# One more Sinkhorn column sum in a fused attention and mixture-of-experts kernel, with the third group of y multiplied one phase later and W2's splits three products later

## The chip, the cores and the metric

The kernel runs on one NeuronCore of a Trainium2 chip, in one launch. The metric is the device time of one execution in microseconds (us); what is shown is the median of several executions. The profile is that of one execution.

## The reference

```python
# linear attention: 4 batches, 8 heads, 768 steps, head size 48
for t in range(S):
    cur = np.einsum('bhd,bhe->bhde', u[None] * kt, vt)
    y[:, :, t] = np.einsum('bhd,bhde->bhe', rt, state + cur)
    state = wt[:, :, :, None] * state + np.einsum('bhd,bhe->bhde', kt, vt)
...
x = np.ascontiguousarray(attn_out.transpose(0, 2, 1, 3)).reshape(B * S, H * D)  # 3072 tokens x 384
a = x @ w1
b = x @ w2
h = a * b @ w3
x = h @ w_out
...
N, D = x.shape
E = w_gate.shape[1]                          # 8 experts, F = 1024
logits = x @ w_gate
logits = logits - logits.max()
P = np.exp(logits)
for _ in range(8):
    P /= P.sum(1, keepdims=True) + 1e-09     # rows
    P /= P.sum(0, keepdims=True) + 1e-09     # columns
    P *= N / E
out = np.zeros((N, D), dtype=np.float32)
for e in range(E):
    h = np.maximum(x @ w1[e], 0.0)
    ye = h @ w2[e]
    out += P[:, e:e + 1] * ye
```

## The kernel before

The attention and the first gated layers take the first 440 us. The rest, the eight experts, is what the change touches. It is cut into 64 phases n = 4k + sb: sb is one of four blocks of 768 tokens, k one of 16 pairs of 128-column slices of the hidden layer (an expert e has two such pairs, e = k // 2). `phase(n)` computes x @ w1 of its slice and block; the second multiplication, with w2, of phase n follows inside phase n + 1, and a 65th phase has only that.

**The first multiplication** (tile `zp`) is done by a scheme that needs 15 products instead of a full set of block products. They come in the order 8, 9, 10, 5, 2, 13, 11, 6, 3, 15, 12, 7, 1, 14, 4. Numbers are split into a high and a low part (fp32r), so a product is 6 matmuls: 128 x 128 weights, 256 moving columns. Around the products ScalarE copies some out of PSUM (L1015, `ct`: that of product 8 must be done before product 9 goes on in the same bank), VectorE adds and subtracts (L1008, L1011), ScalarE makes the high part of relu(.) (L1000, `hh`) and VectorE its low part (L1005, `hl`).

**The second multiplication** (tile `yp`, "y") of a phase has 36 steps of 3 matmuls of the same shape. Three groups b_ = 0, 2, 1 (a group is one 256-column part of the block's tokens) have twelve steps each, and fill two PSUM banks of three. `y_out` adds a finished bank to the accumulator: for e > 0 VectorE multiplies it by the transposed token weights (`yw`, L1191; `pb` is a row of them, broadcast), and GpSimd adds it (L1193). For the first expert it is copied or added without the weights, which are not known yet, and in phases 8 to 11 `rescale` (L1276) multiplies the accumulator by them afterwards.

**What sets the order.** The schedule is written out by hand: each engine runs its instructions in the order in which the program issues them. `after(r)` runs behind each product: tasks that are due, one entry of the list `ex`, at products 2, 4, 6, 8 and 10 of a phase one entry of the list `sk`, and then a number of y steps given by a table (5, 4, 0, 5, 4, 0, 2, 1, 2, 1, 3, 3, 2, 1, the rest). `ex` holds what comes one for a product: the rescalings, and in phases with sb = 2 the splits of two new w2 slices (L740 on ScalarE for the high part, L741 on VectorE for the low one). `sk` holds the Sinkhorn iteration in small pieces, over phases 1 to 7:

```python
def sk_cols():
    pc = pools["y"].tile([P, E], F32, tag="col", name="pcs")
    mm(pc, so["ones"], so["cs"], True, True)
```

is the column sum of one iteration, a plain fp32 matmul with 8 moving columns on TensorE (two instructions in the trace); eight of them fall into phases 2 to 6, and two transposes (`ptn`) of the token weights follow in phase 7. Every matmul of the kernel goes through one helper, L113, so the tiles' names tell them apart.

Of the kernel before, what the change touches and what calls it, by code (L numbers as in the profile page):

```python
# [11 lines left out]
F32 = mybir.dt.float32  # L12
# [46 lines left out]
def tile_rwkv_moe_sinkhorn_moe(  # L59
# [21 lines left out]
    P = 128  # L81
    FF = moe_w3.shape[0] * P
    E = e_w2.shape[0] * 2 * P // FF
# [10 lines left out]
    KD = DM // P  # L94
# [89 lines left out]
    pools = {}  # L184
# [682 lines left out]
    for k in range(NC):  # L867
# [9 lines left out]
        if k + 2 < NC:  # L877
            n = FU + 2 * k + 4
# [80 lines left out]
    so = {}  # L959
# [78 lines left out]
    def phase(n):  # L1038
        z = n < N
        bk, ct = {}, {}  # L1040

        def prod(nm, r, start=False, stop=False):
            if start:
                bk[nm] = z_new()
            z_prod(bk[nm], n, r, start, stop)

        def after(r):
            if ORDER.index(r) % 4 == 3 or r == ORDER[-1]:
                release(n, GOF[r])
            while at["slot"] in due:  # L1050
                for f in due.pop(at["slot"]):
                    f()
            at["slot"] += 1
            if ex:
                ex.popleft()()
            if sk and at["sk"] and ORDER.index(r) in SKP:
                sk.popleft()()
            if n == 0:
                i_ = ORDER.index(r)
                if i_ < PO:  # L1060
                    moe_x2(NB - 1, i_, PO, PARTS[i_:i_ + 2])
                if i_ == PO - 1:
                    open2()
                if i_ == 11:
                    y_fill(0)
                y_units((0, 0, 3, 3, 6)[max(0, i_ - 10)])
            elif n == 1:
                y_units(YN1[r])
            else:
                y_units(YN[r])  # L1070

        def s8():
            prod("b", 8, True, True)
            ct["8"] = cp(bk["b"])

        def s9():
            prod("b", 9, False, True)
            ct["12"] = cp(bk["b"])

        def s10():  # L1080
            prod("b", 10, False, True)
            ct["02"] = cp(bk["b"])

        def s5():
            prod("a", 5, True, True)
            ct["01"] = new_c()
            sub(ct["01"], bk["a"], ct["02"])

        def s2():
            prod("a", 2, False, True)  # L1090
            sub(ct["8"], bk["a"], ct["8"])

        def s13():
            prod("a", 13, False, True)
            ct["00"] = cp(bk["a"])

        def s11():
            prod("g", 11, True, True)
            sub(ct["02"], ct["02"], bk["g"])

        def s6():
            prod("e", 6, True, True)
            ct["10"] = new_c()
            add(ct["10"], ct["00"], bk["e"])

        def s3():
            prod("g", 3, False, True)
            add(ct["00"], ct["00"], bk["g"])

        def s15():  # L1110
            prod("f", 15, True, True)
            sub(ct["10"], ct["10"], bk["f"])
            h_hi(n, 1, 0, ct["10"])
            add(ct["12"], ct["12"], bk["f"])

        def s12():
            prod("h", 12, True, True)
            add(ct["00"], ct["00"], bk["h"])
            h_hi(n, 0, 0, ct["00"])
            h_lo(n, 1, 0)  # L1120

        def s7():
            prod("e", 7, False, True)
            add(ct["8"], ct["8"], bk["e"])
            h_hi(n, 1, 1, ct["8"])
            h_lo(n, 0, 0)

        def s1():
            prod("h", 1, False, True)
            add(ct["12"], ct["12"], bk["h"])  # L1130
            h_lo(n, 1, 1)

        def s14():
            prod("d", 14, True, True)
            add(ct["02"], ct["02"], bk["d"])
            h_hi(n, 0, 2, ct["02"])
            add(ct["12"], ct["12"], bk["d"])
            h_hi(n, 1, 2, ct["12"])

        def s4():  # L1140
            prod("i", 4, True, True)
            add(ct["01"], ct["01"], bk["i"])
            h_hi(n, 0, 1, ct["01"])
            h_lo(n, 0, 2)

        for r, f in zip(ORDER, (s8, s9, s10, s5, s2, s13, s11, s6, s3, s15, s12, s7, s1, s14, s4)):
            if z:
                f()
            after(r)
        if z:  # L1150
            h_lo(n, 1, 2)
            h_lo(n, 0, 1)

    pbc = {}

    def ld_pb(e, sb):
        t = pools["m2"].tile([P, S], F32, tag="pb", bufs=4, name="pb")
        nc.sync.dma_start(t, pd.rearrange("(e t) c -> e (t c)", e=E)[e, sb * S:(sb + 1) * S].partition_broadcast(P))
        pbc[e, sb] = t

    def y_fill(n):
        k, sb = divmod(n, NS)
        e, dp = divmod(k, NDP)
        bank = {}

        def unit(b_, d, i, j):
            first = i == 1 and j == 0
            last = i == 0 and j == 1
            if first and d != 1:
                bank[b_, d // 2] = pools["y"].tile([P, 2, T], F32, tag="y", bufs=3, name="yp")  # L1170
            yp = bank[b_, d // 2]
            hh, hl = hb[n, i, b_]
            wh, wl = w2c[2 * k + j]
            for c, (w_, a_) in enumerate(((wh, hh), (wh, hl), (wl, hh))):
                mm(yp[:, d % 2, :], w_[:, i, d * P:(d + 1) * P], a_[:, j, :], first and c == 0 and d != 1,
                   last and c == 2, skip=True)
            if last and d:
                y_out(yp[:, 0:d % 2 + 1, :], b_, slice(0, 2) if d == 1 else slice(2, 3))

        def y_out(yp, b_, ds):  # L1180
            if k == 0 and sb not in acc:
                acc[sb] = pools["x"].tile([P, KD, S], F32, tag="xa", bufs=NS, name="acc")
            dst = acc[sb][:, ds, b_ * T:(b_ + 1) * T]
            w_ = ds.stop - ds.start
            if k == 0:
                nc.scalar.activation(dst, yp, AF.Copy)
            elif e == 0:
                add(dst, yp, dst)
            else:
                t = pools["m2"].tile([P, w_, T], F32, tag=f"yw{w_}", name="yw")  # L1190
                nc.vector.tensor_tensor(t, yp, pbc[e, sb][:, b_ * T:(b_ + 1) * T].unsqueeze(1).to_broadcast([P, w_, T]),  # L1191
                                        op=ALU.mult)
                (nc.vector if n == N - 1 else nc.gpsimd).tensor_tensor(dst, dst, t, op=ALU.add)  # L1193
            if k == NB2 - 1:
                nc.sync.dma_start(out.rearrange("(d p) t -> p d t", p=P)[:, ds, sb * S + b_ * T:sb * S + (b_ + 1) * T], dst)

        for b_ in (0, 2, 1):
            for d in range(KD):
                for i in (1, 0):
                    for j in range(2):  # L1200
                        yq.append(lambda b_=b_, d=d, i=i, j=j: unit(b_, d, i, j))

    def release(n, g):
        if n >= N:
# [63 lines left out]
        nc.vector.tensor_copy(so["pt"][:, h, :], pt)  # L1268
        nc.sync.dma_start(pd[PH * h:PH * (h + 1), :], so["pt"][:, h, :])

    sk.extend([sk_last, lambda: sk_turn(0), lambda: sk_turn(1), lambda: ld_pb(0, 0)])

    def rescale(sb, d, h):
        ts_ = slice(h * S // 2, (h + 1) * S // 2)
# [8 lines left out]
    for n in range(N + 1):  # L1283
        k, sb = divmod(n, NS)
        if n > 1:
            y_fill(n - 1)
        if n < N:
            if n == 0:
                for m, at_ in enumerate(sorted(hook)):
                    later(m, *hook[at_])  # L1290
                later(4, lambda: sp_w2(0))
                later(6, lambda: sp_w2(1))
                for r, (d0, d1, d2, sb_, ws) in XAT.items():
                    task = lazy(lambda r=r, sb_=sb_, ws=ws: pre_x(NS - 1, r, x2[sb_], ws, nc.gpsimd))
                    for d, f in zip((d0, d1, d2), task):
                        later(d, f)
            if 2 * NS <= n < 3 * NS:
                ex.extend([lambda sb=sb, d=d, h=h: rescale(sb, d, h) for d in range(KD) for h in range(2)])
                if sb < NS - 1:
                    later(2, lambda sb=sb: ld_pb(0, sb + 1))  # L1300
            if n >= 2 * NS:
                later(3, lambda n=n: ld_pb(n // NS // NDP, n % NS))
            if n == 2:
                for g in range(NGR):
                    later(3 * g + 7, lambda g=g: spread(0, 5, sp_w1(2, g, nc.gpsimd)))
            if sb == 1 and k > 0:
                for g in range(NGR):
                    later(3 * g + 1, lambda i=2 * k + 2, g=g: spread(0, 2, sp_w1(i, g, nc.gpsimd)))
            if sb == 2:
                ex.extend([lambda i=i: sp_w2(i) for i in (2 * k + 2, 2 * k + 3)])  # L1310
        at["sk"] = n >= 1
        phase(n)
# [72 lines left out]
```

## Time and profile before

| | |
|---|---|
| median of 3 executions | 1942.75 us (1942.31 to 1945.38) |
| the profiled execution, its own time | 1941.5 us |
| its span | 1939.8 us |
| granted TensorE clock, mean | 1.00 |
| TensorE busy | 1913.2 us, 99% of the span |
| VectorE busy | 1400.1 us, 72% |
| GpSimd busy | 1020.2 us, 53% |
| ScalarE busy | 690.9 us, 36% |

The span is the time from the first to the last instruction of the profiled execution; it lies 1.7 us below that execution's own time. Busy shares are means over the whole program; a matmul's record overlaps with those of its neighbours, so the pace of TensorE is read from the distances between the starts.

### The profile page before, as it was taken

Reading aid. Unit: us, or ns where it says so; the run is one execution under the profiler, and the core shown is the slowest. Engines: PE = TensorE matmul, PEld = TensorE weight load, DVE = VectorE, ACT = ScalarE, POOL = GpSimd, SP = SyncE. Lnnn points to the kernel's source line nnn. Section 1 sums busy time; section 2 is a strip of 40 time slices with the busy share of each in tenths; the row PEclk is TensorE's granted clock in tenths of the full one; section 3 lists DMA queues with packets and bytes.
Section 4 is the critical chain, followed back from the end, with each engine's and each line's share of the span. In section 5 each row is a group of like instructions: output and inputs, shape, how many; then the busy total and the mean of one; then the engine's idle time right before and its main releaser. Section 6 shows DMA issues by size and latency. Waiting matters only on the chain.

```text
span 1939.8 us, 44922 instructions
## 1 busy us (share of the span) xinstructions
PE 1913.2 (99%) x18451; PEld 1879.3 (97%) x18451; DVE 1400.1 (72%) x2424; ACT 690.9 (36%) x1366; POOL 1020.2 (53%) x1245
## 2 busy tenths in 40 slices
PE   6999999999999999999999999999999999999999
PEld 4799999999999999999999999999999999999999
DVE  8866778766687877676767676767677777767666
ACT  6733343445432333333333333333333333323321
POOL 6867666545422455555555545464646464555521
PEclk9999999999999999999999999999999999999999
DMA  9632445349555665565655565556565655555564
GB/s 374 226 106 64 153 132 154 103 146 319 186 208 180 226 222 205 195 218 191 217 188 204 194 219 196 205 198 215 189 218 199 209 201 197 205 192 210 183 212 134
DMA packets 102733, 377.90 MB, mean 195 GB/s; under 512 B 11552, under 2 KB 39040, under 8 KB 76928
## 3 DMA queue, kind: packets, MB, share of 16 engines
q1 hardware_dynamic: 101664, 374.59, 55.0%
q8 instruction: 145, 2.38, 0.5%
q10 hardware_dynamic: 864, 0.44, 0.1%
q14 instruction: 60, 0.49, 0.1%
HBM read 353.26 MB, written 20.55 MB: 193 GB/s over the span
## 4 chain that ended last, share of the span: by engine, by line
PE 92%; DVE 3%; DMA 1%; ACT 1%; POOL 1%; issue 1%; SPq 0%; ACTq 0%; DVEq 0%; POOLq 0%
PE yp L113 41%; PE zp L113 34%; PE po L113 5%; PE pb L113 4%; PE pa L113 4%; PE w34ps L113 1%; PE yt L113 1%; PE sc L113 1%; DMA nat_kn<-in_kn_dram 1%; PE trn L113 0%; DMA raw<-in_moe_w_dram 0%; DVE ct L1008 0%; DMA xraw<-xraw 0%; DVE Sn L456 0%; DVE tx L673 0%
## 5 line engine op out<-in xcount | busy, mean ns | idle before, releaser
L113 PE MATMUL zp<-xc,w1c 128*128 128x256 f32 x5760 | 812.9, 281 | 0.8 <-DVE ct L1008 0.7
L113 PEld LDWEIGHTS zp<-xc,w1c 128*128 128x128 f32 x5760 | 737.4, 189 | 1.4 <-DVE ct L1008 0.9
L1193 POOL TENSOR_TENSOR acc<-acc,yw 128x512 f32<-128x512 f32 x330 | 362.2, 1098 | 561.8 <-DVE yw L1191 558.5
L113 PE MATMUL yp<-hh,w2h 128*128 128x256 f32 x2304 | 647.8, 281 | 0.0
L113 PE MATMUL yp<-hl,w2h 128*128 128x256 f32 x2304 | 647.0, 281 | 0.2 <-DVE hl L1005 0.2
L113 PE MATMUL yp<-hh,w2l 128*128 128x256 f32 x2304 | 646.8, 281 | 0.0
L113 PEld LDWEIGHTS yp<-hh,w2l 128*128 128x128 f32 x2304 | 441.4, 192 | 0.0
L113 PEld LDWEIGHTS yp<-hh,w2h 128*128 128x128 f32 x2304 | 432.9, 188 | 0.2 <-issue 0.2
L113 PEld LDWEIGHTS yp<-hl,w2h 128*128 128x128 f32 x2304 | 432.5, 188 | 0.5 <-DVE hl L1005 0.4
L1000 ACT ACTIVATE hh<-ct 128x512 fp32r<-128x512 f32 x384 | 236.1, 630 | 539.5 <-DVE ct L1011 272.8
L1008 DVE TENSOR_TENSOR ct<-ct,zp 128x512 f32<-128x512 f32 x576 | 381.1, 679 | 41.0 <-PE zp L113 37.7
L1005 DVE SCALAR_TENSOR_TENSOR hl<-ct,hh 128x512 fp32r<-128x512 f32 x384 | 314.6, 833 | 0.0
L1015 ACT ACTIVATE ct<-zp 128x512 f32<-128x512 f32 x256 | 152.5, 596 | 446.3 <-PE zp L113 446.3
L1191 DVE TENSOR_TENSOR yw<-yp,pb 128x512 f32<-128x512 f32 x336 | 185.6, 552 | 85.7 <-issue 22.1
L1011 DVE TENSOR_TENSOR ct<-ct,zp 128x512 f32<-128x512 f32 x128 | 87.9, 687 | 166.9 <-PE zp L113 166.9
L681 POOL TENSOR_TENSOR w1c<-w1s,w1c 128x512 fp32r<-128x512 f32 (+1 forms) x120 | 127.8, 1065 | 101.9 <-ACT w1c L677 101.9
L1011 DVE TENSOR_TENSOR ct<-zp,ct 128x512 f32<-128x512 f32 x128 | 88.3, 690 | 117.0 <-PE zp L113 101.0
L673 POOL TENSOR_TENSOR w1s<-w1raw 128x128 f32<-128x128 f32 x240 | 127.0, 551 | 0.2
L545 POOL TENSOR_TENSOR gl<-gs,gh 128x256 fp32r<-128x256 f32 (+1 forms) x88 | 81.2, 926 | 78.7 <-ACT gh L541 78.5
L113 PE MATMUL pb<-xhl,w2h 128*128 128x256 f32 (+1 forms) x528 | 103.9, 291 | 1.3 <-DVE gs L536 0.9
L113 PE MATMUL pa<-xhl,w1h 128*128 128x256 f32 (+1 forms) x528 | 102.7, 289 | 1.7 <-ACT w34s L263 1.0
L681 POOL TENSOR_TENSOR w1c<-w1raw,w1c 128x128 fp32r<-128x128 f32 (+1 forms) x93 | 59.0, 635 | 66.6 <-ACT w1c L677 64.9
(197 smaller groups left out, 2116.3 us busy)
## 6 DMA issues: line engine op xcount, KB each, us to landing
xc<-xd SPq DMA_DIRECT2D x192, 1024.0 KB, 4.9
xc<-xd SPq DMA_DIRECT2D x64, 768.0 KB, 4.3
pb<-pd SPq DMA_DIRECT2D x60, 384.0 KB, 5.7
xd<-x2s SPq DMA_DIRECT2D x54, 256.0 KB, 2.7
w1raw<-in_e_w_dram SPq DMA_DIRECT2D x32, 384.0 KB, 3.1
w2raw<-in_e_w_dram SPq DMA_DIRECT2D x32, 384.0 KB, 3.7
raw<-in_moe_w_dram SPq DMA_DIRECT2D x8, 1024.0 KB, 8.6
nat_w<-in_w_dram SPq DMA_DIRECT2D x24, 264.5 KB, 3.7
```

Source lines behind the costliest of these rows:

```text
L113: nc.tensor.matmul(o, lhsT, rhs, start=start, stop=stop, **kw)
L545: nc.gpsimd.tensor_tensor(gl[:, f, :], m_t.pop(("gs", blk, f)), gh[:, f, :].bitcast(F32), op=ALU.subtract)
L673: eng.tensor_tensor(tmp_[:, many.index(r), :], at_(a), at_(b), op=ALU.add if sg == 1 else ALU.subtract)
L681: eng.tensor_tensor(lo[:, d0:d1, :], sv, hi[:, d0:d1, :].bitcast(F32), op=ALU.subtract)
L1000: nc.scalar.activation(hh, src, AF.Relu)
L1005: nc.vector.scalar_tensor_tensor(hl, src, 0.0, hh.bitcast(F32), op0=ALU.max, op1=ALU.subtract)
L1008: nc.vector.tensor_tensor(o, a, b_, op=ALU.add)
L1011: nc.vector.tensor_tensor(o, a, b_, op=ALU.subtract)
L1015: nc.scalar.activation(t, src, AF.Copy)
L1191: nc.vector.tensor_tensor(t, yp, pbc[e, sb][:, b_ * T:(b_ + 1) * T].unsqueeze(1).to_broadcast([P, w_, T]), op=ALU.mult)
L1193: (nc.vector if n == N - 1 else nc.gpsimd).tensor_tensor(dst, dst, t, op=ALU.add)
```

## The change

Three things are done. One: a piece `sk_edge` is added at the end of `sk`. It is one more column sum, the same matmul as in `sk_cols` into a tile that nobody reads; it stands behind the two transposes and the load of the first broadcast weights, in phase 7 behind product 6. Two: the results of the third group (b_ = 1) of y(n) are not handed to `y_out` in phase n + 1, where the group is computed, but kept, and taken behind products 8 and 9 of phase n + 2; the steps of that group are sorted so that the three d of i = 1 come before those of i = 0. Three: `ex` gets three empty entries ahead, so that the rescalings stand behind products 5 to 3 instead of 8 to 13, and the two W2 splits behind products 5 and 2 instead of 8 and 9 (in phase 10, where the rescalings are ahead of them, behind 15 and 12 instead of 11 and 6).

On TensorE in phase 7 of the changed kernel (`zp` the products, `yp` the y steps, `pcs` the new sum; the numbers are those of the weights' buffers):

```order
L113 MATMUL yp<-hl,w2h_7526 128x256
L113 MATMUL yp<-hh,w2l_7527 128x256
L113 MATMUL zp<-xc_8861,w1c_7641 128x256 x3
L113 MATMUL zp<-xc_8861,w1c_7918 128x256 x3
L113 MATMUL pcs<-cs,ones 128x8
L113 MATMUL yp<-hh,w2h_7494 128x256
```

The sum stands between the six matmuls of product 6 and the y step that follows it; the rows around it are in before in the same order.

On VectorE at the end of one of the later phases and the start of the next, before (`yw` is the multiplication by the weights, `ct` the additions around the products, `hl` the low parts):

```order
L1008 TENSOR_TENSOR ct<-ct,zp 128x512
L1005 SCALAR_TENSOR_TENSOR hl<-ct,hh 128x512
L1191 TENSOR_TENSOR yw<-yp,pb 128x512
L1008 TENSOR_TENSOR ct<-ct,zp 128x512 x3
L1005 SCALAR_TENSOR_TENSOR hl<-ct,hh 128x512
L1191 TENSOR_TENSOR yw<-yp,pb 128x256
L1005 SCALAR_TENSOR_TENSOR hl<-ct,hh 128x512 x2
L1191 TENSOR_TENSOR yw<-yp,pb 128x512
L1011 TENSOR_TENSOR ct<-zp,ct 128x512
```

and the same place after the change:

```order
L1008 TENSOR_TENSOR ct<-ct,zp 128x512
L1005 SCALAR_TENSOR_TENSOR hl<-ct,hh 128x512
L1008 TENSOR_TENSOR ct<-ct,zp 128x512 x3
L1005 SCALAR_TENSOR_TENSOR hl<-ct,hh 128x512 x3
L1198 TENSOR_TENSOR yw<-yp,pb 128x512
L1198 TENSOR_TENSOR yw<-yp,pb 128x256
L1198 TENSOR_TENSOR yw<-yp,pb 128x512
L1011 TENSOR_TENSOR ct<-zp,ct 128x512
```

The two multiplications of the third group (a wide and a narrow one) stood ahead of the last additions and among the low parts; they now stand behind all of these, next to the first multiplication of the new phase.

On VectorE in phase 10, before (`acc` the rescalings, `w2l` the low parts of the W2 splits):

```order
L1276 TENSOR_TENSOR acc<-acc,pb 128x384 x2
L1011 TENSOR_TENSOR ct<-ct,zp 128x512
L741 TENSOR_TENSOR w2l_10072<-w2raw,w2h_10071 128x768
L1191 TENSOR_TENSOR yw<-yp,pb 128x512
L1008 TENSOR_TENSOR ct<-ct,zp 128x512
L741 TENSOR_TENSOR w2l_10098<-w2raw,w2h_10097 128x768
```

and after:

```order
L1289 TENSOR_TENSOR acc<-acc,pb 128x384
L1011 TENSOR_TENSOR ct<-ct,zp 128x512
L1008 TENSOR_TENSOR ct<-ct,zp 128x512
L741 TENSOR_TENSOR w2l_10123<-w2raw,w2h_10122 128x768
L1198 TENSOR_TENSOR yw<-yp,pb 128x256
L1008 TENSOR_TENSOR ct<-ct,zp 128x512
L1005 SCALAR_TENSOR_TENSOR hl<-ct,hh 128x512
L741 TENSOR_TENSOR w2l_10147<-w2raw,w2h_10146 128x768
```

The rescalings reach further into the phase, and the two low parts of W2 stand three products later, among the additions that end in h. The diff:

```diff
--- before.py
+++ after.py
@@ -1045,6 +1045,8 @@
             z_prod(bk[nm], n, r, start, stop)
 
         def after(r):
+            if r in ORDER[:2] and kept:
+                kept.popleft()()
             if ORDER.index(r) % 4 == 3 or r == ORDER[-1]:
                 release(n, GOF[r])
             while at["slot"] in due:
@@ -1152,6 +1154,7 @@
             h_lo(n, 0, 1)
 
     pbc = {}
+    kept = deque()
 
     def ld_pb(e, sb):
         t = pools["m2"].tile([P, S], F32, tag="pb", bufs=4, name="pb")
@@ -1175,7 +1178,11 @@
                 mm(yp[:, d % 2, :], w_[:, i, d * P:(d + 1) * P], a_[:, j, :], first and c == 0 and d != 1,
                    last and c == 2, skip=True)
             if last and d:
-                y_out(yp[:, 0:d % 2 + 1, :], b_, slice(0, 2) if d == 1 else slice(2, 3))
+                f = lambda: y_out(yp[:, 0:d % 2 + 1, :], b_, slice(0, 2) if d == 1 else slice(2, 3))
+                if b_ == 1 and n < N - 1:
+                    kept.append(f)
+                else:
+                    f()
 
         def y_out(yp, b_, ds):
             if k == 0 and sb not in acc:
@@ -1195,10 +1202,12 @@
                 nc.sync.dma_start(out.rearrange("(d p) t -> p d t", p=P)[:, ds, sb * S + b_ * T:sb * S + (b_ + 1) * T], dst)
 
         for b_ in (0, 2, 1):
-            for d in range(KD):
-                for i in (1, 0):
-                    for j in range(2):
-                        yq.append(lambda b_=b_, d=d, i=i, j=j: unit(b_, d, i, j))
+            pieces = [(d, i) for d in range(KD) for i in (1, 0)]
+            if b_ == 1 and n < N - 1:
+                pieces.sort(key=lambda x: -x[1])
+            for d, i in pieces:
+                for j in range(2):
+                    yq.append(lambda b_=b_, d=d, i=i, j=j: unit(b_, d, i, j))
 
     def release(n, g):
         if n >= N:
@@ -1268,7 +1277,11 @@
         nc.vector.tensor_copy(so["pt"][:, h, :], pt)
         nc.sync.dma_start(pd[PH * h:PH * (h + 1), :], so["pt"][:, h, :])
 
-    sk.extend([sk_last, lambda: sk_turn(0), lambda: sk_turn(1), lambda: ld_pb(0, 0)])
+    def sk_edge():
+        pc = pools["y"].tile([P, E], F32, tag="col", name="pcs")
+        mm(pc, so["ones"], so["cs"], True, True)
+
+    sk.extend([sk_last, lambda: sk_turn(0), lambda: sk_turn(1), lambda: ld_pb(0, 0), sk_edge])
 
     def rescale(sb, d, h):
         ts_ = slice(h * S // 2, (h + 1) * S // 2)
@@ -1295,6 +1308,7 @@
                     for d, f in zip((d0, d1, d2), task):
                         later(d, f)
             if 2 * NS <= n < 3 * NS:
+                ex.extend([lambda: None] * 3)
                 ex.extend([lambda sb=sb, d=d, h=h: rescale(sb, d, h) for d in range(KD) for h in range(2)])
                 if sb < NS - 1:
                     later(2, lambda sb=sb: ld_pb(0, sb + 1))
@@ -1307,6 +1321,8 @@
                 for g in range(NGR):
                     later(3 * g + 1, lambda i=2 * k + 2, g=g: spread(0, 2, sp_w1(i, g, nc.gpsimd)))
             if sb == 2:
+                if not ex:
+                    ex.extend([lambda: None] * 3)
                 ex.extend([lambda i=i: sp_w2(i) for i in (2 * k + 2, 2 * k + 3)])
         at["sk"] = n >= 1
         phase(n)
```

## Rows read from the trace of the kernel before

**Rows 1.** The page, busy time by engine (part 1) and costliest group (part 5).

```profile
PE 1913.2 (99%) x18451; PEld 1879.3 (97%) x18451; DVE 1400.1 (72%) x2424; ACT 690.9 (36%) x1366; POOL 1020.2 (53%) x1245
...
L113 PE MATMUL zp<-xc,w1c 128*128 128x256 f32 x5760 | 812.9, 281 | 0.8 <-DVE ct L1008 0.7
```

**Rows 2.** The chain of waits, two neighbouring phases: start us, us, what.

```profile
758.02 1.77 PE yp L113 x15
...
781.35 1.77 PE yp L113 x15
```

**Rows 3.** Timeline of TensorE, phase 5: start us, us, engine, line, operation, tiles, shapes.

```profile
558.38 0.28 PE L113 MATMUL yp<-hh,w2h 128*128 128x256 f32 x1
...
572.20 0.28 PE L113 MATMUL yp<-hh,w2l 128*128 128x256 f32 x1
```

**Rows 4.** Three windows: us; busy us of PE, PEld, DVE, ACT, POOL (records); clock; DMA.

```profile
559.00:572.00 13.00, 13.00 (x117) 13.00 (x117) 12.80 (x25) 4.72 (x11) 8.05 (x14) 1.00 0.64 228
584.00:596.00 12.00, 12.00 (x104) 12.00 (x103) 10.94 (x20) 4.17 (x7) 0.00 (x0) 1.00 0.68 234
758.02:781.35 23.33, 23.33 (x201) 23.33 (x200) 18.14 (x30) 8.13 (x14) 6.46 (x6) 1.00 0.66 224
```

**Rows 5.** Timeline of TensorE around three column sums and a transpose, phases 2 to 7.

```profile
488.02 0.29 PE L113 MATMUL pcs<-cs,ones 128*128 128x8 f32 x2
...
488.95 0.28 PE L113 MATMUL yp<-hh,w2h 128*128 128x256 f32 x1
...
503.57 0.28 PE L113 MATMUL pcs<-cs,ones 128*128 128x8 f32 x2
...
503.91 0.28 PE L113 MATMUL yp<-hl,w2h 128*128 128x256 f32 x1
...
513.34 0.29 PE L113 MATMUL pcs<-cs,ones 128*128 128x8 f32 x2
...
596.87 0.27 PE L113 MATMUL ptn<-ident,L 128*96 128x128 f32 x1
```

**Rows 6.** Timeline at the start of phase 6: VectorE, ScalarE, weight load [idle before <- releaser].

```profile
567.82 1.21 DVE L1005 SCALAR_TENSOR_TENSOR hl<-ct,hh 128x512 fp32r<-128x512 f32 x1
...
568.95 0.68 DVE L1008 TENSOR_TENSOR acc<-yp,acc 128x512 f32<-128x512 f32 x1
...
571.34 0.68 DVE L1005 SCALAR_TENSOR_TENSOR hl<-ct,hh 128x512 fp32r<-128x512 f32 x1
...
571.99 0.58 ACT L1015 ACTIVATE ct<-zp 128x512 f32<-128x512 f32 x1
...
572.62 0.19 PEld L113 LDWEIGHTS zp<-xc,w1c 128*128 128x128 f32 x1 [0.34 <-ACT ct L1015]
```

**Rows 7.** Timeline of phase 18: ScalarE and TensorE at its start, VectorE at its end.

```profile
852.03 0.58 ACT L1015 ACTIVATE ct<-zp 128x512 f32<-128x512 f32 x1
...
852.91 0.87 PE L113 MATMUL zp<-xc,w1c 128*128 128x256 f32 x6
...
871.63 0.69 DVE L1191 TENSOR_TENSOR yw<-yp,pb 128x512 f32<-128x512 f32 x1
```

**Rows 8.** Timeline of VectorE in phase 18, and TensorE's product 13.

```profile
856.72 0.69 DVE L1011 TENSOR_TENSOR ct<-zp,ct 128x512 f32<-128x512 f32 x1
857.77 0.42 DVE L1191 TENSOR_TENSOR yw<-yp,pb 128x256 f32<-128x256 f32 x1 [0.37 <-PE yp L113]
859.12 0.69 DVE L1011 TENSOR_TENSOR ct<-zp,ct 128x512 f32<-128x512 f32 x1 [0.92 <-PE zp L113]
...
860.33 0.64 PE L113 MATMUL zp<-xc,w1c 128*128 128x256 f32 x4
```

**Rows 9.** Timeline of ScalarE and VectorE in phase 10, the splits of W2.

```profile
675.22 1.57 ACT L740 ACTIVATE w2h<-w2raw 128x768 fp32r<-128x768 f32 x2
...
676.09 0.96 DVE L741 TENSOR_TENSOR w2l<-w2raw,w2h 128x768 fp32r<-128x768 f32 x1
```

**Rows 10.** Timeline of VectorE in phase 6, the first of four small Sinkhorn operations.

```profile
577.42 0.35 DVE L1245 TENSOR_TENSOR Pm<-Pm,cs 128x192 f32<-128x192 f32 x1
```

## The prediction

> **What bounds the kernel now.** I read the engine table first: TensorE is busy for 99% of the span, VectorE for 72% [rows 1]. The reader should see that no other engine can be the bound of the whole, and that 5,760 product matmuls waited 0.8 us in all. The chain of waits confirms it for the expert stage: one group of y steps after another on TensorE, and the same place in two neighbouring phases is 781.35 − 758.02 = 23.33 us apart [rows 2]. A phase is 198 matmuls (15 products of 6 and 36 steps of 3), so one starts every 117.8 ns. Nothing waits; so the time can only change through the number of matmuls, through new waits, or through the pace itself.
>
> The pace is what I looked at next, start by start in the timeline of TensorE. Between 558.38 and 572.20 lie 122 matmuls of the same shape: 113.3 ns each [rows 3]. That is another pace than the 117.8 ns of later phases. The windows show the same: 117 records in 13.00 us ahead of 572, 104 in 12.00 us from 584 on, both at a granted clock of 1.00, which is the 2.4 GHz level [rows 4]. So it is not the granted clock. I call the two paces fast and slow. From 584 on the chain repeats itself phase after phase at 23.3 us to the end; the kernel runs at the slow pace for nearly all of the expert stage.
>
> What switches the pace? I followed it from event to event. A column sum (ones times cs, 8 columns) at 488.02 ends a slow stretch: from 488.95 to the next sum at 503.57 there are 129 matmuls, 14.62 us, 113.3 ns each. That sum ends the fast stretch: from 503.91 to the third sum at 513.34 there are 80, 9.43 us, 117.9 ns [rows 5]. The next two flip it as well, and the last of the eight, which lies between the two windows of [rows 4], turned fast into slow. Two of the eight seem to leave the pace fast, and just ahead of each TensorE had stopped: for one of them weights waited 0.34 us for a copy [rows 6]. I read that as a stop that may flip the pace too, so that the sum flips it back. The 96-column transpose at 596.87 [rows 5] and its twin 3 us later lie in a slow stretch and leave it slow. In steady phases, where neither stops nor such odd matmuls occur, I found no flip.
>
> **The change, part by part.**
>
> *The added column sum* stands in phase 7 after the transposes, where the pace of before is slow. Its own price: from 503.57 to 503.91 is 0.34 us for a sum and one ordinary matmul of 0.113 [rows 5], so 0.23 us. It waits for nothing and nobody reads it. If it flips the pace as the others did, what follows runs at the fast pace: 7 products of 6 and 16 steps of 3 in phase 7 make 90, phases 8 to 63 make 56 × 198 = 11,088, the last y 108; together 11,286 matmuls. At 117.8 − 113.3 = 4.5 ns each [rows 2, 3] that is −50.8 us. Bounds: 0, if the sum flips nothing, and −50.8.
>
> *The third group's multiplications* leave the boundary of a phase. At the end of phase 18 one of them takes VectorE from 871.63 on for 0.69 us, just ahead of the three additions which the last groups of h wait for; ScalarE makes these groups before it copies product 8 of the next phase [rows 7]. The tightest phases are those of token block 2: at the start of phase 18 this copy ran from 852.03 to 852.61 and product 9's matmuls began at 852.91, so 0.3 us of room at the slow pace, 0.2 if the weights are counted, which load one matmul earlier. At the fast pace TensorE comes to this point 0.9 us per phase earlier, while the VectorE work is as long as before: with the old order I would expect a stop there, as the one in phase 6, where an accumulation stood at 568.95 among the same operations, and the weights of 572.62 waited 0.34 us for the copy of 571.99 [rows 6]. The change takes 0.69 from that queue, about the fast pace's whole need. I cost the moved multiplications at 0 in themselves: VectorE works 18.14 of 23.33 us in a phase [rows 4], and they now run while the first products do. If that cover is gone, they delay the subtraction that product 13 needs. The stop of phase 6 goes: −0.3 (572.62 − 572.20 − 0.113), between 0 and −0.3.
>
> *W2's splits three products later.* In phase 18 the splits stood at the phase's start. Now the first comes behind the subtraction that begins at 856.72 and ahead of the one at 859.12, on which product 13 at 860.33 waits [rows 8]. Between them are 859.12 − 857.41 = 1.71 us, and some 0.4 behind; a split takes 0.96 [rows 9], the narrow multiplication 0.42: hidden, 0. In phase 10 the splits stand behind the rescalings, now behind products 15 and 12, where VectorE has additions to do for the next products. A split's subtraction waits there for ScalarE, which takes 1.57 for two high parts, and takes 0.96 itself [rows 9]. At the fast pace product 15 ends after 129 × 0.1133 = 14.6 us of the phase and product 1 starts after 162 × 0.1133 = 18.36; between stand a start of 0.2, 1.2 for two additions, 0.55 for the high part of h, 0.8 for a split's, 0.9 for its low part, 0.3 and 0.6 for a multiplication and the addition waited for: 18.8 instead of 18.25. That is a first stop of about 0.55; the two behind it I estimate alike, 0.5 and 0.75: +1.8 in all, between 0 and 3 (1.2 at the slow pace). In phase 6 the second split's low part comes together with Sinkhorn's four small operations from 577.42 on, at 0.35 or less each [rows 10]: about +0.2 at product 13, between 0 and 1.
>
> *Before the new sum*, if phase 6 no longer stops, its first sum turns fast into slow for what lies up to the next one, at most (584 − 572.62) / 0.1178 = 97 matmuls: 97 × 4.5 ns = +0.4.
>
> **The sum:** −50.8 + 0.23 − 0.3 + 1.8 + 0.2 + 0.4 = −48.5. The profiled execution took 1941.5 us (its span 1939.8 and 1.7 around it), so 1893.0; the median of the runs is 1.25 above that execution, so 1894.3.
>
> The Trainium skill, "TensorE: Matmul & The Clock Gate", section "Back-to-back issue gap", gives one gap for a width of moving columns at the upper clock level, 262 cycles for 256 columns, 109 ns. The rows have two gaps, 113.3 and 117.8, for one and the same shape and clock, so its rule is not the whole story; by it the second pace would not exist and the sum would be that of the last rival below. The section "LDWEIGHTS (loading the stationary operand)" says that a load goes by its columns, 128 / 1.2 = 107 ns, which is nearer to the fast pace; no row says why the slow one is longer.
>
> **The rivals.**
>
> *Slow to the end.* A sum flips whichever pace it finds. If the pace ahead of the new one is fast, because phase 6 has lost one stop or gained one, or the transposes behave otherwise from the fast side, the sum turns it slow. For: each removed stop changes the parity, and a stop flips only about half the time. Against: before, the place was slow, and a lost stop with a won one leave it so. Then the costs remain: +0.23 − 0.3 + 1.2 + 0.2 + 0.4 = +1.7, 1944.5 (1943 with the sum alone).
>
> *Fast for a part.* The stops in phase 10, or a rare late copy at a boundary, flip the pace back. With the fast pace for half of the matmuls: −25.4 + 2 gives about 1919. For: 0.3 us of room [rows 7], and VectorE fuller at the fast pace. Against: the 0.69 us freed.
>
> *Slower.* The split overtakes: in 14 phases of token block 2 the low part now stands ahead of the subtraction for product 13. It decides if split and multiplication there exceed 1.71 + 0.4 = 2.1 us. Unhindered they are 0.96 + 0.42 = 1.4; but a VectorE operation can be stretched: the same hl took 1.21 at 567.82 and 0.68 at 571.34 [rows 6], 1.78 times. So stretched they take 2.45 and product 13 waits 0.35, 14 times: +4.9, with the slow pace and its +1.7: 1949.4. Against: it needs the stretch in most of these phases and the slow pace as well.
>
> *No second pace to win.* If the gaps of the two stretches came from their surroundings and not from a state that lasts, only +0.23 and the stops remain, about 1943. Against it stand eleven thousand matmuls at 117.8 without a change. This is the time by the skill's one gap for a width, with which the trace disagrees.
>
> **How the numbers follow.** Fast to the end 0.50, slow to the end 0.27, fast for a part 0.12, slower 0.08, no second pace 0.03. What a measurement can tell from no change here is 0.2%, 3.9 us. Faster: 0.50 and 0.10 of the part-time case (the rest of it ends within 0.2%), 0.60; the same 0.27 + 0.02 + 0.03 = 0.32; slower 0.08. The likeliest gives 1894.3, its own range 1889 (no stops, a few more fast matmuls) to 1905 (phase 10 flips the pace for some phases). Half of the chance lies elsewhere, so the range reaches over the part-time case to the slow one with all of its costs: 1889 to 1946; only the slower case and little of the others stay outside.
>
> **What would show it.** In the profile after: phases 22.44 us apart (198 × 113.3) instead of 23.33; the mean record of a product's matmul near 276 ns instead of 281 [rows 1]; in the timeline, starts 117.8 apart ahead of the new sum and 113.3 behind it; no wait for the copy at 572; a wait of about half a microsecond for VectorE in phase 10. Wrong would make it: starts at 117.8 behind the new sum, or a flip at one of the stops later on.

## The result, and the profile after

The changed kernel takes 1898.42 us in the median of four executions (1896.76, 1898.00, 1898.85 and 1945.71), the kernel before 1943.30 on the same chip. The ratio is 0.9765, 95% interval 0.9746 to 0.9784. The ratios of this document leave out executions more than 1.5% above the fastest of their kernel, here the one at 1945.71, although by what follows it is one that did not end at the faster pace; the medians count them. Forecast were 1894.3 us and a range of 1889 to 1946.

The profiled execution took 1896.76 us, its span is 1895.0. The page of the changed kernel, busy time by engine and the product matmuls (line, engine, tiles, count; busy us, mean ns; idle before them), answers to [rows 1]:

```profile
PE 1867.1 (99%) x18453; PEld 1832.2 (97%) x18453; DVE 1375.2 (73%) x2424; ACT 698.4 (37%) x1366; POOL 986.4 (52%) x1245
...
L113 PE MATMUL zp<-xc,w1c 128*128 128x256 f32 x5760 | 791.6, 277 | 3.3 <-DVE ct L1008 2.1
```

TensorE is as full as before, with two more records, but a product's matmul has 277 ns instead of 281, and its idle time has risen from 0.8 to 3.3 us: faster and with more waits. The chain of waits at the place of [rows 2], now three phases in a row:

```profile
757.72 1.70 PE yp L113 x15
...
780.16 1.70 PE yp L113 x15
...
802.60 1.70 PE yp L113 x15
```

They are 22.44 us apart: 198 matmuls at 113.3 ns. Before they were 23.33 apart. Where it begins is seen in the timeline of TensorE in phase 7, with the new sum:

```profile
607.32 0.40 PE L113 MATMUL zp<-xc,w1c 128*128 128x256 f32 x2
607.55 0.28 PE L113 MATMUL pcs<-cs,ones 128*128 128x8 f32 x2
607.69 0.36 PE L113 MATMUL yp<-hh,w2h 128*128 128x256 f32 x1
607.89 0.28 PE L113 MATMUL yp<-hl,w2h 128*128 128x256 f32 x1
```

and in windows of the changed kernel around it and in phases 10 to 12 (us, busy us of TensorE with its records, granted clock, DMA share, GB/s):

```profile
594.00:606.00 12.00, 12.00 (x104) 1.00 0.54 184
609.00:621.00 12.00, 12.00 (x108) 1.00 0.65 237
670.00:680.00 10.00, 10.00 (x91) 1.00 0.69 247
693.00:706.00 13.00, 13.00 (x113) 1.00 0.52 193
710.00:722.00 12.00, 12.00 (x109) 1.00 0.28 89
```

A window counts every record that overlaps it, two or three more than start in it. In 12 us there are 104 records ahead of the sum and 108 behind it, at the same granted clock of 1.00, the 2.4 GHz level. From 693 to 706 the pace is slow once more (113 in 13 us, where 117 stood in [rows 4]), then fast to the end. What borders that stretch are stops of TensorE; the timeline of phases 10 and 11, with the idle time and what ended it:

```profile
665.55 0.77 PEld L113 LDWEIGHTS zp<-xc,w1c 128*128 128x128 f32 x6 [0.33 <-ACT ct L1015]
...
682.96 0.39 PE L113 MATMUL zp<-xc,w1c 128*128 128x256 f32 x1 [1.14 <-DVE ct L1008]
...
690.69 0.39 PE L113 MATMUL zp<-xc,w1c 128*128 128x256 f32 x1 [0.99 <-ACT ct L1015]
...
707.79 0.39 PE L113 MATMUL zp<-xc,w1c 128*128 128x256 f32 x1 [0.23 <-DVE ct L1008]
```

The late weights at 665.55 and the stop of 1.14 left the pace fast, that of 0.99 left it slow, that of 0.23 fast again. So in this execution the fast pace behind the sum lasted from 607.55 to 690.69; the one that holds to the end, 10,438 starts 113.3 ns apart, came with the stop at 707.79. The stop of 1.14 has its cause on VectorE and ScalarE in phase 10, to be set beside [rows 9]:

```profile
679.51 0.68 DVE L1008 TENSOR_TENSOR ct<-ct,zp 128x512 f32<-128x512 f32 x1
681.02 0.96 DVE L741 TENSOR_TENSOR w2l<-w2raw,w2h 128x768 fp32r<-128x768 f32 x1 [0.84 <-ACT w2h L740]
681.89 0.42 DVE L1198 TENSOR_TENSOR yw<-yp,pb 128x256 f32<-128x256 f32 x1
682.23 0.68 DVE L1008 TENSOR_TENSOR ct<-ct,zp 128x512 f32<-128x512 f32 x1
```

VectorE stands idle for 0.84 us until ScalarE has made the high part of W2, then makes the low part and a multiplication, and only then the addition of 682.23, for which product 1 at 682.96 waits. That is the queue which the prediction described.

### The profile page after: what moved, and what is told of

It is laid out like the page before. It is cut to its first block, busy times and chain, and to the rows that moved or that the text cites. A ratio compares the mean times of both kernels' runs of the same rounds, so it can differ in the third digit from the quotient of the medians.

```text
span 1895.0 us, 44944 instructions
## 1 busy us (share of the span) xinstructions
PE 1867.1 (99%) x18453; PEld 1832.2 (97%) x18453; DVE 1375.2 (73%) x2424; ACT 698.4 (37%) x1366; POOL 986.4 (52%) x1245
## 4 chain that ended last, share of the span: by engine, by line
PE 92%; DVE 4%; ACT 1%; DMA 1%; issue 1%; POOL 1%; SPq 0%; DVEq 0%; ACTq 0%; POOLq 0%
PE yp L113 40%; PE zp L113 34%; PE po L113 5%; PE pb L113 4%; PE pa L113 4%; PE w34ps L113 1%; PE yt L113 1%; PE sc L113 1%; DVE ct L1008 1%; DMA nat_kn<-in_kn_dram 1%; PE trn L113 0%; DMA raw<-in_moe_w_dram 0%; DVE Sn L456 0%; DVE hl L1005 0%; DVE cvp L237 0%
## 5 line engine op out<-in xcount | busy, mean ns | idle before, releaser
L113 PE MATMUL zp<-xc,w1c 128*128 128x256 f32 x5760 | 791.6, 277 | 3.3 <-DVE ct L1008 2.1
L113 PEld LDWEIGHTS zp<-xc,w1c 128*128 128x128 f32 x5760 | 716.8, 188 | 4.6 <-DVE ct L1008 2.7
L113 PE MATMUL yp<-hh,w2h 128*128 128x256 f32 x2304 | 638.0, 277 | 0.0
L113 PE MATMUL yp<-hl,w2h 128*128 128x256 f32 x2304 | 637.2, 277 | 0.2 <-DVE hl L1005 0.2
L1200 POOL TENSOR_TENSOR acc<-acc,yw 128x512 f32<-128x512 f32 x330 | 338.8, 1034 | 573.5 <-DVE yw L1198 572.0
L113 PE MATMUL yp<-hh,w2l 128*128 128x256 f32 x2304 | 636.9, 276 | 0.0
L113 PEld LDWEIGHTS yp<-hh,w2l 128*128 128x128 f32 x2304 | 432.6, 188 | 0.0
L1005 DVE SCALAR_TENSOR_TENSOR hl<-ct,hh 128x512 fp32r<-128x512 f32 x384 | 280.7, 757 | 0.0
L1198 DVE TENSOR_TENSOR yw<-yp,pb 128x512 f32<-128x512 f32 x336 | 181.2, 552 | 98.2 <-POOL acc L1200 59.7
L113 PEld LDWEIGHTS pa<-xhl,w1h 128*128 128x128 f32 x528 | 82.7, 188 | 2.5 <-ACT w34s L263 1.1
```

The lines of the kernel that those rows point to most:

```text
L113: nc.tensor.matmul(o, lhsT, rhs, start=start, stop=stop, **kw)
L1005: nc.vector.scalar_tensor_tensor(hl, src, 0.0, hh.bitcast(F32), op0=ALU.max, op1=ALU.subtract)
```

## The experiments

The theory was that of the prediction: the pace of TensorE is a state with two levels, a column sum flips it, a stop may flip it, and otherwise it lasts. The rival was that the new order on VectorE gives the time. Twelve kernels were run, in four groups; the table has every execution.

| kernel | executions, us | ratio to before (interval) |
|---|---|---|
| no_sum | 1898.16, 1899.12, 1899.84, 1900.20 | 0.9774 (0.9760 to 0.9789) |
| sum_only | 1895.52, 1895.70, 1914.90, 1944.12 | 0.9788 (0.9737 to 0.9839) |
| two_sums | 1898.32, 1900.24, 1900.82, 1900.93 | 0.9778 (0.9763 to 0.9793) |
| sums_7_36 | 1921.52, 1921.83, 1922.46, 1923.12 | 0.9891 (0.9874 to 0.9907) |
| splits_first | 1896.09, 1896.45, 1897.54, 1941.33 | 0.9760 (0.9744 to 0.9777) |
| no_sum_sf | 1895.02, 1895.71, 1898.96, 1949.57 | 0.9760 (0.9743 to 0.9776) |
| transpose_sf | 1897.87, 1898.26, 1942.60, 1946.06 | 0.9767 (0.9748 to 0.9787) |
| sum_kept | 1893.50, 1893.60, 1893.89, 1938.10, 1941.83 | 0.9744 (0.9725 to 0.9764) |
| sum_12_moves | 1895.19, 1895.46, 1897.37, 1897.44 | 0.9756 (0.9741 to 0.9770) |
| moves_only | ten, 1941.88 to 1944.00 | 0.9996 (0.9987 to 1.0006) |
| sum_12_only | 1899.17, 1899.37, 1899.88, 1900.62 | 0.9774 (0.9758 to 0.9790) |
| ordinary_12 | ten, 1941.70 to 1944.56 | 0.9999 (0.9989 to 1.0008) |

**The sum taken away (no_sum).**

```diff
-    sk.extend([sk_last, lambda: sk_turn(0), lambda: sk_turn(1), lambda: ld_pb(0, 0), sk_edge])
+    sk.extend([sk_last, lambda: sk_turn(0), lambda: sk_turn(1), lambda: ld_pb(0, 0)])
```

> The changed kernel without the added sum; the moved multiplications and splits stay. Theory 1, that the sum flips a pace which then lasts: the starts stay 117.8 ns apart behind phase 7, and the time is that of the kernel before plus the costs of the moves, about 1944 us (1942 to 1946). Rival, that the new order of VectorE gives the pace or the time: about 1898, or some part of the 45 us.

Measured: 1899.48. The expectation failed: without the sum the kernel is nearly as fast. By the time alone the rival would have won. The windows of its TensorE, and the first of the three stops between them:

```profile
612.00:632.00 20.00, 20.00 (x173) 1.00 0.53 182
716.00:736.00 20.00, 20.00 (x179) 1.00 0.60 204
```

```profile
686.70 0.38 PE L113 MATMUL zp<-xc,w1c 128*128 128x256 f32 x1 [0.85 <-DVE ct L1008]
```

The pace stays slow behind phase 7 (173 in 20 us), as theory 1 says, up to the first stop of phase 10, and is fast behind it (179). So the stops that the change makes in phase 10 are a second way to the fast pace. Only a kernel without sum and without stops could tell the two theories apart.

**The sum alone, at its place (sum_only).**

```diff
+    def sk_edge():
+        pc = pools["y"].tile([P, E], F32, tag="col", name="pcs")
+        mm(pc, so["ones"], so["cs"], True, True)
...
-    sk.extend([sk_last, lambda: sk_turn(0), lambda: sk_turn(1), lambda: ld_pb(0, 0)])
+    sk.extend([sk_last, lambda: sk_turn(0), lambda: sk_turn(1), lambda: ld_pb(0, 0), sk_edge])
```

> The kernel before with the added sum alone; multiplications and splits at their old places. Theory 1: starts 113.3 ns apart behind the sum in phase 7. If the old order then stops TensorE at the starts of the phases of token block 2, as I predicted, the profile has some fourteen stops of about 0.3 us, and each may flip the pace: somewhere between 1900 and 1940, about 1920. If the moves aren't needed for the pace, about 1897 (without phase 10's stops even 1895). Rival, the order alone: 1943.

Measured: two executions at 1895.6, one at 1914.9, one at 1944.1. The profile is of the last. Its windows, and the start of phase 10:

```profile
620.00:640.00 20.00, 20.00 (x179) 1.00 0.65 220
680.00:700.00 20.00, 20.00 (x172) 1.00 0.67 235
```

```profile
668.24 0.58 ACT L1015 ACTIVATE ct<-zp 128x512 f32<-128x512 f32 x1
...
668.87 0.30 PEld L113 LDWEIGHTS zp<-xc,w1c 128*128 128x128 f32 x2 [0.18 <-ACT ct L1015]
```

The sum made it fast; 2.5 phases later the copy of product 8 was 0.18 us late, the stop that I expected at the fast pace, and behind it the pace is slow to the end. That such a stop flips in some executions and not in others is not shown here, since the other three have no profile, but their times fit it. I had expected 1900 to 1940, or 1895 to 1897 if the moves are not needed: one execution fits the first, two the second and one neither, so what the sum alone gives at this place stays unclear.

**Two sums (two_sums, sums_7_36).** The changed kernel with a second sum, a product after the first one's next, and 29 phases later:

```diff
-    sk.extend([sk_last, lambda: sk_turn(0), lambda: sk_turn(1), lambda: ld_pb(0, 0), sk_edge])
+    sk.extend([sk_last, lambda: sk_turn(0), lambda: sk_turn(1), lambda: ld_pb(0, 0), sk_edge, sk_edge])
...
+    sk.extend([sk_last, lambda: sk_turn(0), lambda: sk_turn(1), lambda: ld_pb(0, 0), sk_edge] + [lambda: None] * 144 + [sk_edge])
```

> The changed kernel with a second sum of the same kind in phase 7, one product behind the first one's next (behind product 15). Theory 1, each sum flips: fast for about 20 matmuls between the two, then slow to the end, about 1944 us. Rival, a sum sets the fast pace whatever it finds: still about 1898.

> The changed kernel with a second sum 29 phases later, in phase 36 behind product 6, amid steady phases. Theory 1: fast from phase 7 to phase 36, slow from there to the end: 27.5 phases of 198 matmuls at 4.5 ns more, +24.5 on 1898, about 1922 us, with phases 22.44 us apart ahead of it and 23.32 behind. Rival, a sum sets the fast pace: 1898. Rival, the flips belong to the Sinkhorn stage's own traffic and not to the sum: 1898 too.

Measured: 1900.53 and 1922.14. In the first, the timeline of TensorE shows the second sum at 612.21, and what follows it:

```profile
610.17 0.85 PE L113 MATMUL zp<-xc,w1c 128*128 128x256 f32 x6
610.85 0.28 PE L113 MATMUL yp<-hh,w2h 128*128 128x256 f32 x1
...
612.21 0.28 PE L113 MATMUL pcs<-cs,ones 128*128 128x8 f32 x2
```

```profile
614.00:634.00 20.00, 20.00 (x173) 1.00 0.51 171
716.00:736.00 20.00, 20.00 (x178) 1.00 0.59 195
```

From 610.17 to 612.21 there are 18 matmuls 113.3 ns apart; from 614 on the pace is slow. So the second sum flipped back, as theory 1 has it, and the time of 1944 that I drew from it was missed for the reason seen in no_sum: phase 10's stops made it fast again. In the other kernel nothing stops TensorE any more where the second sum stands, and time and windows (ahead and behind it) come out as forecast:

```profile
1240.00:1262.00 22.00, 22.00 (x196) 1.00 0.43 151
1268.00:1290.00 22.00, 22.00 (x189) 1.00 0.53 185
```

This shows the flip away from the Sinkhorn stage: a matmul of 8 columns that nobody reads costs 24 us, since the fast pace is lost behind it.

**Phase 10 without its stops (splits_first, no_sum_sf, transpose_sf).** The splits of phase 10 go ahead of the rescalings; then with the sum, without it, and with a third transpose in its place:

```diff
-                ex.extend([lambda i=i: sp_w2(i) for i in (2 * k + 2, 2 * k + 3)])
+                for m, i in enumerate((2 * k + 2, 2 * k + 3)):
+                    ex.insert(3 + m, lambda i=i: sp_w2(i))
...
-        pc = pools["y"].tile([P, E], F32, tag="col", name="pcs")
-        mm(pc, so["ones"], so["cs"], True, True)
+        pt = pools["y"].tile([PH, P], F32, tag="col", name="ptn")
+        mm(pt, L.rearrange("p t e -> p (t e)")[:, :PH], ident, True, True, tr=True)
```

> The changed kernel, but in phase 10 the two W2 splits go ahead of the rescalings (behind products 5 and 2, as in the other phases of block 2). The sum in phase 7 stays. Theory 1 (sums flip the pace, and a stop of TensorE can flip it too): the stops of phase 10, 3 us in the changed kernel, go and with them their flips; fast from phase 7 on, about 1895.5 us. Rival, that the fast pace comes from phase 10's stops alone and the sum's flip is undone somewhere on the way: about 1943.

> The same without the sum: the moved multiplications and splits, the splits of phase 10 ahead of the rescalings. Theory 1: without the sum and without phase 10's stops nothing flips the pace behind phase 7, so it stays slow, about 1944 us (1942 to 1946), though the kernel without the sum took 1899.5. Rival, that the new order of VectorE itself gives the time: about 1896.

> The same with one more 96-column transpose of the token weights in the sum's place, no reader. The two transposes of phase 7 flipped nothing in any profile so far. Theory 1, that the kind of matmul matters: slow, about 1944 us. Rival, that any matmul that breaks the row of like ones, or their odd number, flips the pace: about 1896.

Measured: 1896.99, 1897.34 and 1920.43, each a mixture of about 1897 and 1941 to 1950. The edit took away the long stops but not all: in no_sum_sf one of 0.23 us is left, in phase 11, between slow (172 in 20 us) and fast (179):

```profile
612.00:632.00 20.00, 20.00 (x172) 1.00 0.56 200
716.00:736.00 20.00, 20.00 (x179) 1.00 0.69 235
```

```profile
706.77 0.39 PE L113 MATMUL zp<-xc,w1c 128*128 128x256 f32 x1 [0.23 <-DVE ct L1008]
```

transpose_sf has the same, with slow windows behind its third transpose: that transpose flipped nothing. In the profile of splits_first, an execution of 1941.33 us, the pace went from fast to slow at a start that came 0.11 us late (689.12 instead of 689.01, at the start of phase 11), and the same stop in phase 11 left it slow:

```profile
706.00 0.98 PE L113 MATMUL zp<-xc,w1c 128*128 128x256 f32 x6 [0.23 <-DVE ct L1008]
```

So a stop of the same place and size flips the pace in one profile and not in another. As a comparison of times the three decide little, and the forecast of 1944 us without the sum failed in three of the four executions of no_sum_sf.

**The third group's multiplications with the sum, without the later splits (sum_kept).** Rescalings and splits at their old places:

```diff
-                ex.extend([lambda: None] * 3)
...
-                if not ex:
-                    ex.extend([lambda: None] * 3)
```

> The kernel before with the sum and the multiplications of the third group one phase later; the rescalings and splits at their old places. Theory 1: the sum turns the pace fast in phase 7; phase 10 has no stops of half a microsecond. If the multiplications alone make the room that the fast pace needs, about 1895.5 us in each execution; if the splits at the phase's start still make product 8's copy late at the fast pace, stops at the starts of phases of block 2, and times from 1896 to 1930.

Measured: three executions at 1893.7, the fastest of all, and two at 1938 and 1942. The three have no profile; by their times there is nothing of phase 10's 3 us in them. In the profiled execution, of 1941.83 us, the pace was fast up to a start in phase 10 that came 0.09 us late, and slow from there. The six matmuls of that product, of which the second started at 683.42 (0.201 us after the first instead of 0.113), and windows ahead of them and behind:

```profile
683.22 0.95 PE L113 MATMUL zp<-xc,w1c 128*128 128x256 f32 x6
```

```profile
660.00:680.00 20.00, 20.00 (x179) 1.00 0.64 224
690.00:710.00 20.00, 20.00 (x172) 1.00 0.51 182
```

**The clean test (sum_12_moves, moves_only, sum_12_only).** In the profiles all flips but the sums' lay in phases 8 to 11 or ahead of them. So these phases got the old order, in which the slow pace has no stops, and the sum went behind them, into phase 12; the multiplications of the third group and the later splits (from phase 14 on) stay in the first two:

```diff
-                ex.extend([lambda: None] * 3)
...
-                if not ex:
+                if k > 2:
                     ex.extend([lambda: None] * 3)
...
+    sk.extend([sk_last, lambda: sk_turn(0), lambda: sk_turn(1), lambda: ld_pb(0, 0), lambda: None] + [lambda: None] * 21 + [sk_edge])
```

> The kernel before with the third group's multiplications one phase later, W2's splits three products later from phase 14 on, phases 8 to 11 in the old order, and the sum not in phase 7 but in phase 12 behind product 9. Theory 1: up to phase 12 the slow pace stops nowhere, so every execution comes to the sum at the slow pace and leaves it at the fast one, with the order that has room for it: 10,400 matmuls at 4.5 ns less, about -46.5: 1897 us in each execution, none near 1943. Rival, that the pace ahead of the sum differs between executions by itself: a mixture of 1897 and 1943.

> The same without the sum. Theory 1: no event flips the pace behind phase 7, 1943 us in each execution (1942 to 1945). Rival, that the moves themselves shorten the time: below 1940.

> The kernel before with the sum in phase 12 alone, multiplications and splits at their old places. Theory 1: each execution is fast behind the sum, and the late copies at the starts of phases of block 2 (stops of 0.1 to 0.3 us, which the slow pace hasn't) flip it at some of them: times scattered from 1898 to 1940, about 1915. If the moves are not needed to keep the pace: 1897 in each execution.

Measured: 1896.42 in four like executions, 1942.38 in ten like ones, 1899.62 in four like ones. The windows of sum_12_moves ahead of and behind its sum at 715.45, and the same two of moves_only:

```profile
690.00:710.00 20.00, 20.00 (x172) 1.00 0.51 185
720.00:740.00 20.00, 20.00 (x179) 1.00 0.68 237
```

```profile
690.00:710.00 20.00, 20.00 (x172) 1.00 0.50 183
720.00:740.00 20.00, 20.00 (x172) 1.00 0.68 237
```

One column sum is the difference between 1942.4 and 1896.4. The order on VectorE alone gives nothing (ratio 0.9996). In sum_12_only the late copies of block 2 are there, a like one in twelve of the phases behind the sum; the first:

```profile
758.69 0.30 PEld L113 LDWEIGHTS zp<-xc,w1c 128*128 128x128 f32 x2 [0.19 <-ACT ct L1015]
```

None of the twelve flipped the pace in the profile, nor, by their times, in the other three executions; so this expectation was half wrong. By the distances between the starts each costs 0.26 us (758.42 to 758.91 for two matmuls instead of 0.227), so the twelve make up the 3.2 us that lie between the two kernels: that is what the moves give, once the pace is fast.

**One more ordinary matmul (ordinary_12).** The same place, another kind:

```diff
-        pc = pools["y"].tile([P, E], F32, tag="col", name="pcs")
-        mm(pc, so["ones"], so["cs"], True, True)
+        pc = pools["y"].tile([P, T], F32, tag="col", name="pcs")
+        g = GOF[10]
+        mm(pc, w1c[6, g][:, 0, WP_[g][4][10], :], xc[12, g][:, 0, XP_[g][4][10], :], True, True)
```

> As the version with the sum in phase 12, but in the sum's place one more matmul of the ordinary kind (split fp32r, 128 x 128 weights, 256 columns, parts of the next product's operands, no reader). If it is the sum's kind, fp32 in two passes and 8 columns, that flips the pace: no flip, 1942.4 us as the moves alone. Rival, that one matmul more or less in the row is what counts (odd number): about 1896.5.

Measured: 1943.45, ten like executions. One more matmul in the row isn't it; the kind is. A sum also leaves a late start behind it, which the ordinary matmul does not: the second start behind the sum comes after 0.20 us (607.69 to 607.89 in the changed kernel). But behind a transpose it is the same 0.20 (597.81 to 598.01), and every transpose that came at the slow pace left it slow, 28 in the fourteen traces; so this late start alone does not make the flip. Whether the 8 columns, the plain fp32 or the two instructions of the sum do, no run separates.

## Why the prediction was right, and where its sum was off

*The mechanism held, but not all the way in this kernel.* The sum flips slow to fast, the fast pace is 113.3 ns, and it lasts where no stop comes: shown by the changed kernel's own windows, by sums_7_36 on both sides, and by the pair sum_12_moves and moves_only. The fourteen traces have 122 column sums. Of these, 106 have no late start among the eighteen matmuls ahead of them, and every one turned the pace round, 52 from slow to fast and 54 from fast to slow; the other 16 have a start 0.02 to 0.3 us late a few matmuls ahead. The rule of the Trainium skill that I set against it ("TensorE: Matmul & The Clock Gate", section "Back-to-back issue gap", one gap for a width) would have left the time at 1943; the trace has both gaps in one execution. The 262 cycles stand there for an isolated matmul; for a stream of weight loads and matmuls the section says that both set the spacing, and it gives none for 256 columns.

*The sum, 1893.0 against 1896.76 of the profiled execution.* Behind phase 12 a phase gains 0.89 us, as forecast. The term that was mis-sized is that of the stops in phases 10 and 11: +1.8 was taken, with 3 as its bound. The stops measure 1.14, 0.99 and 0.23 as recorded, 2.4; by the starts of the stopped matmul and the one behind it they cost 1.4, 1.3 and 0.5, with a fourth of 0.4 at the start of phase 10: 3.6, over the bound. Part of this was a slip of addition: the terms for the first stop make 19.15 and not 18.8, so a stop of 0.9 and not 0.55. The slow stretch between 691 and 708, which I had put into a rival and not into the sum, costs 139 matmuls at 4.5 ns, 0.6. The stage before the sum lost 0.9 us (the first transpose went from 596.87 to 597.78) instead of 0.3. A matmul gains 4.45 ns and not 4.5, which is 0.6 over all of them. Together these are +3.6 of the 3.8.

*What the prediction had wrong is the part of the stops.* It booked phase 10's as a cost and as a danger to the fast pace, and named a flip at one of them as a sign of being wrong; the profile has two such flips, at 690.69 and 707.79. The stops are also a second way to the fast pace: in no_sum and two_sums the profiles show the pace in front of them slow and behind them fast, and by their times all eight executions ended fast. So the sum is sufficient (sum_12_moves) but in this kernel not necessary, and "slow to the end" needs that both fail. Without the sum the change gives 1899.48 instead of 1898.42. That the time came out near the forecast is therefore partly luck: had the stop at 707.79 not turned the pace back, 10,438 matmuls at 4.45 ns would have made the profiled execution 46 us longer (an estimate), about as long as the one of 1945.71.

*Whether the sum finds the slow pace* was the largest doubt, 0.27. I argued that the number of stops in phase 6 decides it. In all profiles the pace behind the two transposes was slow, and moves_only shows why the stops don't matter. Windows of it ahead of the first transpose and behind it, and the transpose:

```profile
585.00:597.00 12.00, 12.00 (x108) 1.00 0.69 240
598.00:600.30 2.30, 2.30 (x22) 1.00 0.09 21
```

```profile
597.48 0.27 PE L113 MATMUL ptn<-ident,L 128*96 128x128 f32 x1
```

Here the pace came fast (108 in 12 us) and left the transpose slow: its starts behind are 117.9 ns apart, with no stop there. In the other profiles it came slow and stayed so. A transpose of this kind thus leaves the slow pace from either side, as far as one case can show it, and the sum right behind it finds the same pace in all the profiles. It fits that the kernel before, which has nothing behind the transposes, was slow in all of its executions.

*The rivals.* Fast for a part is, by its time, what sum_only did in one execution (1914.9), and the profile of the changed kernel has a slow part of 139 matmuls. Slow to the end, or nearly so, happened in one of four of the changed kernel's (1945.71). Which event lost the pace in that one isn't shown, since the profile is of another execution; in splits_first and sum_kept profiles of such executions show it lost at a start that came 0.1 us late in phase 10 or 11. The slower case, a split that delays product 13, isn't in the trace: no stop stands in the later phases of block 2.

*What stays open* is why the slow pace has 4.5 ns more, and which stops flip: one of 0.18 did at the start of phase 10 in sum_only, twelve of the same form and size later did not in sum_12_only, and that of 0.23 in phase 11 went either way.

The version with the sum behind phases 8 to 11 is at least as fast as the changed kernel (0.9756 against 0.9765, intervals that overlap), and its four executions lie within 2.3 us. It gives away the gain of phases 7 to 12, some 4 us, for coming to the sum without stops.

## What to carry to other kernels

When one engine is busy all the time, compare the distances between its starts in different stretches before looking for waits: a row of like matmuls can run at two paces at the same granted clock. A change of a few per cent with no wait that went may be a flip of this pace; look for the odd matmul or the stop at which it begins, and compare single executions, not medians alone. To tell a cause from a second way to the same effect, take away both: the kernel without the sum was nearly as fast, and only two kernels without the stops, one with the sum and one without it, showed what the sum does.

## What the runs showed of the hardware that was not expected

- 128 x 128 weights with 256 fp32r columns start 113.3 or 117.8 ns apart at the granted clock of 1.00, for thousands of matmuls in a row.
- An fp32 matmul of 8 columns (two instructions) flipped the pace from slow to fast and from fast to slow: in two_sums at 609.59 and 612.21, and 29 phases later in sums_7_36. A 96-column transpose took fast to slow once (moves_only) and left slow as it was; one more ordinary matmul did nothing (ordinary_12).
- At a start that came 0.09 us late in sum_kept the pace flipped for the rest of the program; that execution took 48 us more than three others of the same kernel. A stop of 0.23 us in phase 11 turned slow into fast in the changed kernel and left slow as it was in splits_first.
